# Step A of the first batch behind 22 idle matmuls, four of its groups in three fp32r parts, and no idle matmuls ahead of step D

## The chip, the cores and the metric

The kernel runs on one core of one Trainium2 chip. Its engines are TensorE (PE, with its weight loads shown as PEld), VectorE (DVE), ScalarE (ACT), GpSimd (POOL) and SyncE (SP, which here only issues DMAs). The metric is the device time of one execution in microseconds, and of several runs the median. Times inside a trace are counted from the first instruction of the span.

## What is computed

The reference mixes each sequence in the frequency domain and then runs a two-layer network over all tokens:

```python
X = np.fft.rfft(x, axis=1)                     # x: 4 x 3008 x 256
Yr = Xr @ w_r - Xi @ w_i + b_r
Yi = Xr @ w_i + Xi @ w_r + b_i
Yr = np.sign(Yr) * np.maximum(np.abs(Yr) - lam, 0.0)    # lam = 0.01, the same for Yi
y = np.fft.irfft(Yr + 1j * Yi, n=3008, axis=1)
h = y.reshape(12032, 256) @ w_in               # 256 x 2048
g = np.maximum(h, 0.0) + alpha * np.minimum(h, 0.0)
out = g @ w_out                                # 2048 x 256
```

## The kernel before

**The transform as matmuls.** 3008 = 47 x 64, so the transform and its inverse are each two short DFTs. For a batch b, step A (`a_load`, `a_mm`, `a_evac`) multiplies x by a 47-point table, in 16 groups g of two rows each (`NG = R // 2`). Step B (`b_load`, `b_mm`, `b_evac`, `b_evac2`) does the 64-point part for 12 pairs q, `m_mm` and `m_evac` mix the channels and shrink, step C (`c_mm`, `c_evac`) begins the inverse transform, and step D (`d_load`, `d_open`, `d_step`) ends it and leaves the tokens split into a high and a low fp32r part for the two layers (`l1_step`, `l2_step`), which fill the rest of the time.

**Two ways to multiply.** A product in full float32 is one call in the code and two matmul instructions in the trace. A product in fp32r needs its inputs split into a high and a low part (`split`: ACT copies the high part, another engine subtracts it) and is three instructions: high weight by high data, low weight by high data, high weight by low data. In `a_mm`, batches 0 and 1 take the first way with the table `lf_s` (L389), batches 2 and 3 the second with `la_s` (L392 to L394); for those `a_split` makes the parts `xh` and `xl`, each from two buffers.

**The head of the program** is written out by hand (from L988), and each engine runs its instructions in the order in which they are written. POOL issues the loads of `lf_s`, of the small tables for the bias (`first_bias`, L188 and L191) and of `la_s`. DVE clears the bias tiles (L194, L195) and then the tile `idle`. PE runs `keep_warm(36)`, which is 36 matmuls of 128 x 128 in bf16 of a tile of zeros, whose result nobody reads. SP issues the loads of x: a pair of groups (four rows) is two DMAs, one of 80 partitions and one of 14, and the first pair is four; behind them the tables `rb_s`, the first loads of batch 1 (`xt`), the mixing weights (`wm_f`) and the first raw layer weights (`cw_s`). SP has eight semaphores for its DMAs, so that the ninth DMA waits for the first to land.

**The loop over step A** runs over the 16 groups of batch 0 and the first four (`EARLY`) of batch 1:

```python
for n, (b, g) in enumerate(seq):
    a_mm(b, g)
    if n >= 1:
        a_evac(*seq[n - 1])
    if n == NG:
        for q in range(3):
            b_load(0, q)
```

In batch 0 `a_evac` puts even groups on ACT (L406) and odd ones on DVE (L404); `b_load` is two DMAs on POOL (L420). The products of a group stand in a PSUM tile of the pool `ps_f`, tag "f", which has three buffers: a group writes where the third group before it stood, and waits until that was read. `b_load(0, q)` needs all 16 groups of batch 0, the last of which DVE evacuates. Behind the loop stands `keep_warm(70)` (`WARM`), then the loop over the 12 pairs.

**Ahead of step D**, a list written out by hand (`TAIL`) ends step C, issues the first two loads of step D (`zt`) and fills PE with ten more groups of step A of batch 1; behind them come `keep_warm(12)` and the first two steps D. `d_step` takes two `ps_f` tiles, one for each half of the channels, and each becomes high and low parts on ACT and DVE (L139, L142).

Of the kernel before, what the change touches and what calls it, by code (L numbers as in the profile page):

```python
# [93 lines left out]
def fft_mix_moe(ctx, tc, x, w_r, w_i, b_r, b_i, w_in, w_out, alpha, la, rb, lc, rd, lf, cf, sel, out):  # L94
    nc = tc.nc
# [35 lines left out]
    V, G, A, PE = nc.vector, nc.gpsimd, nc.scalar, nc.tensor  # L131

    def f(t):
        return t.bitcast(F32)

    def split(src, hi, lo, e_hi, e_lo):

        if e_hi is A:
            A.activation(out=hi, in_=src, func=AF.Copy)  # L139
        else:  # L140
            e_hi.tensor_copy(out=hi, in_=src)
        e_lo.tensor_tensor(out=lo, in0=src, in1=f(hi), op=ALU.subtract)  # L142


    la_s = const.tile([NP, 2, NQ], F32R, name="la_s")
# [37 lines left out]
    def first_bias():  # L183

        raw = work.tile([4, 2, C], F32, tag="Yt", name="bias_f", bufs=1)
        hi = work.tile([4, 2, C], F32R, tag="Yc", name="bias_h", bufs=1)
        pick = work.tile([4, 129], F32, tag="ot", name="sel", bufs=1)
        nc.gpsimd.dma_start(out=pick, in_=sel)  # L188
        for i, b in enumerate((b_r, b_i)):
            for k in range(2):  # L190
                nc.gpsimd.dma_start(out=raw[2 * i:2 * i + 2, k], in_=b.unsqueeze(0).to_broadcast([2, C]))  # L191
        rows = const.tile([128, 2, C], F32R, tag="bias", name="bias_p")
        ones = const.tile([128, 128], F32R, tag="wd", name="ones")
        V.memset(f(rows), 0.0)  # L194
        V.memset(f(ones), 0.0)  # L195
        bias[0] = ones, rows

        def parts():
            V.memset(lam_s, -LAM)
            V.tensor_copy(out=ones[0:4], in_=pick[:, 0:128])  # L200
            V.tensor_copy(out=hi, in_=raw)
            V.scalar_tensor_tensor(out=rows[0:4], in0=f(hi), scalar=pick[:, 128:129], in1=raw, op0=ALU.mult, op1=ALU.add)

        return parts
# [9 lines left out]
    def load_rb(n0, n1):  # L214
        nc.sync.dma_start(out=rb_s[:, n0:n1], in_=rb[:, n0:n1])
# [10 lines left out]
    def split_mix():  # L226
        for t, w in zip(mix_w, mix):
            split(t, w[:, 0], w[:, 1], A, G)
        mix_w.clear()
# [24 lines left out]
    def conv_load():  # L254

        m, i = divmod(conv_m[0], 2)
        conv_m[0] += 1
        k = conv_m[0] % 3
        raw = cw_s[:, NSLOT + 8 * k:NSLOT + 8 * k + 8].rearrange("p (k n) f -> p k (n f)", k=2)
        raw = raw.rearrange("p k (n w) -> p k n w", w=2)  # L260
        src = w_out.bitcast(U32)[256 * m:256 * m + 256] if i else w_in.bitcast(U32)[:, 512 * m:512 * m + 512]
        nc.sync.dma_start(out=raw.rearrange("p k n w -> p k (n w)"), in_=src.rearrange("(k p) f -> p k f", p=128))
        conv_raw.append((raw, m, i))
# [77 lines left out]
    def a_load(b, g):  # L341

        if g == 0:
            ad[b] = dram.tile([NQ, R, C], F32, tag="ad", name=f"ad{b}")
        src = x[b].rearrange("(p r) c -> p r c", r=R)[:, 4 * g:4 * g + 4]
        if b == 0:
            ts = [x_s[:, 4 * g:4 * g + 4]]
        elif b == 1 and g in X1_TAGS:
            tags = X1_TAGS[g]
            ts = [work.tile([NP, 4 // len(tags), C], F32, tag=tag, name="xt", bufs={"Yl": None, "gh": 4}.get(tag, 1))  # L350
                  for tag in tags]
        else:
            ts = [work.tile([NP, 4, C], F32, tag="xt", name="xt")]
        if (b, g) == (0, 0):
            ts = [ts[0][:, 0:2], ts[0][:, 2:4]]
        n = 4 // len(ts)
        for i, t in enumerate(ts):

            for p in ((0, 80), (80, NP)):
                nc.sync.dma_start(out=t[slice(*p)], in_=src[slice(*p), n * i:n * i + n])  # L360
        xt[b, g] = ts

    def x_rows(b, g):
        ts = xt[b, g // 2]
        if len(ts) == 1:
            return [ts[0][:, 2 * (g % 2):2 * (g % 2) + 2]]
        n = len(ts) // 2
        return ts[n * (g % 2):n * (g % 2) + n]

    xp = {}  # L370

    def a_split(b, g):

        t, = x_rows(b, g)
        hi = work.tile([NP, 2, C], F32R, tag="xh", name="xh")
        lo = work.tile([NP, 2, C], F32R, tag="xl", name="xl")
        split(t, hi, lo, A, V)
        xp[b, g] = hi, lo
# [3 lines left out]
    def a_mm(b, g):  # L382
        ps = ps_f.tile([NQ, 2, C], F32, tag="f", name="ps_a")
        pa[b, g] = ps
        if b < 2:
            ts = x_rows(b, g)
            n = 2 // len(ts)
            for i, t in enumerate(ts):
                PE.matmul(ps[:, n * i:n * i + n], lf_s, t, start=True, stop=True)  # L389
            return  # L390
        hi, lo = xp.pop((b, g))
        PE.matmul(ps, la_s[:, 0], hi, start=True, stop=False)  # L392
        PE.matmul(ps, la_s[:, 1], hi, start=False, stop=False)
        PE.matmul(ps, la_s[:, 0], lo, start=False, stop=True)  # L394

    def a_evac(b, g):
        ps = pa.pop((b, g))
        if b == 0:
            st = a0_s[:, g]
        else:  # L400
            tag = A1_TAGS[g] if b == 1 and g < len(A1_TAGS) else "zst"
            st = work.tile([NQ, 2, C], F32, tag=tag, name="ast", bufs={"bt": 3, "zst": 3, "Yt": 1, "Yc": 1}.get(tag))
        if b == 0 and g % 2:
            V.tensor_copy(out=st, in_=ps)  # L404
        else:
            A.activation(out=st, in_=ps, func=AF.Copy)  # L406
        if b:
            stores.append((ad[b][:, 2 * g:2 * g + 2], st))
# [3 lines left out]
    def b_load(b, q):  # L412
        t = work.tile([128, 2, C], F32, tag="bt", name="bt", bufs=3)
        if b == 0:
            src = a0_s.rearrange("(w s q) g r c -> q w s (g r) c", w=4, s=2)[q]
        else:
            src = ad[b].rearrange("(w s q) r c -> q w s r c", w=4, s=2)[q]

        for k in range(2):
            (nc.gpsimd if b == 0 else nc.sync).dma_start(out=t[:, k], in_=src[:, k])  # L420
        bt[b, q] = t
# [549 lines left out]
    PAT = [0, 0] + [1] * 46  # L971
    NG = R // 2
    EARLY = 4
    FILL = 14
    C0 = 2
    PT = [1, 2, 3, 3, 3, 3, 3, 3, 3, 3, 4, 4]
# [4 lines left out]
    idle = const.tile([128, 128], BF16, name="idle")  # L981

    def keep_warm(n):
        ps = ps_f.tile([128, 512], F32, tag="f", name="ps_idle")
        for _ in range(n):
            PE.matmul(ps[:, 0:128], idle, idle, start=True, stop=True)

    with tc.manual_schedule():  # L988
        nc.gpsimd.dma_start(out=lf_s, in_=lf)
        bias_parts = first_bias()  # L990
        nc.gpsimd.dma_start(out=la_s, in_=la)
        V.memset(idle, 0.0)
        keep_warm(36)
        for g in range(NG // 2):
            a_load(0, g)
        load_rb(0, 4)
        for g in range(EARLY // 2):
            a_load(1, g)
# [3 lines left out]
        for _ in range(C0):  # L1002
            conv_load()
        seq = [(0, g) for g in range(NG)] + [(1, g) for g in range(EARLY)]

        for n, (b, g) in enumerate(seq):
            a_mm(b, g)
            if n >= 1:
                a_evac(*seq[n - 1])
            if n == NG:  # L1010
                for q in range(3):
                    b_load(0, q)
                split_mix()
                bias_parts()
# [9 lines left out]

        a1 = [EARLY]
        hold = []

        def a_fill(n):
            for g in range(a1[0], min(a1[0] + n, FILL)):
                a_mm(1, g)  # L1030
                a_evac(1, g)
                a1[0] = g + 1
# [38 lines left out]
                {"me": m_evac, "cm": c_mm, "ce": c_evac}[op](0, NPAIR - args[0])  # L1071
        V.tensor_scalar(out=beta_s, in0=alpha_s, scalar1=-1.0, scalar2=1.0, op0=ALU.mult, op1=ALU.add)
        conv_tags.update(v1=("xh", "xl"), ex=("Yh", "Yh"), lf=("Yl", "bt"))
        keep_warm(12)
        for c in range(2):
            d_open(c)
            d_step(0, c)
# [22 lines left out]
        for b in range(B):  # L1100
# [9 lines left out]
            if b == 0:  # L1110
                for g in range(FILL, NG):
                    i = 6 * (g - FILL) + 9
                    if g % 2 == 0:
                        at(i - 8, a_load, 1, g // 2)
                    at(i, a_mm, 1, g)
                    at(i, a_evac, 1, g)
            else:
                for g in range(NG if b + 1 < B else 0):
                    i = AO[b + 1] + 3 * g // 2
                    if g % 2 == 0:  # L1120
                        at(i - 5, a_load, b + 1, g // 2)
                    at(i - 2, a_split, b + 1, g)
                    at(i, a_mm, b + 1, g)
                    at(i, a_evac, b + 1, g)
# [73 lines left out]
        for k in range(len(spairs) + SLAG):  # L1198
# [9 lines left out]
            if k >= SLAG:  # L1208
                n, t = spairs[k - SLAG]
# [43 lines left out]
```

## Time and profile before

| What | us |
|---|---|
| Median of 3 runs (lowest, highest) | 1350.11 (1349.89, 1350.86) |
| The profiled execution | 1351.47 |
| Span of its trace, first to last instruction | 1349.7 |
| PE busy in it | 1334.4 |
| First idle matmul to first matmul of step A | 1.68 to 5.13 |
| First load of step B issued; its first matmul | 20.80; 28.57 |
| First matmul of step D | 101.22 |

The profile was taken in one execution. A row of its timeline gives the start and the length of a run of like instructions, their count, and in brackets how long the engine was idle before them and what ended that. PE's matmuls overlap: one of 512 columns in float32 is listed with some 0.59 us, but the next begins 0.43 us after it. The idle time of an engine that nobody waits for costs nothing.

### The profile page before, as it was taken

The numbers are of one execution on the slowest core, as the hardware profiler recorded it, in microseconds if no ns is written. First come the engines' busy times: TensorE is split into PE (matmuls) and PEld (weight loads), VectorE is DVE, ScalarE is ACT, GpSimd is POOL, SyncE is SP. The second block draws the span as 40 slices with busy tenths as digits, with TensorE's granted clock in tenths as the row PEclk, the third lists the DMA queues.
The fourth block names the chain that finished last, engine by engine and source line by source line (L and its number), as shares of the span: only waits on it lengthen the run. The fifth ranks groups of instructions, "written<-read, shape, count | busy, mean of one in ns | idle before, by whom it ended". The sixth has DMA issues, their size and how long they took to land.

```text
span 1349.7 us, 25116 instructions
## 1 busy us (share of the span) xinstructions
PE 1334.4 (99%) x9200; PEld 1250.5 (93%) x9200; DVE 1035.8 (77%) x1934; ACT 760.9 (56%) x1527; POOL 379.0 (28%) x403
## 2 busy tenths in 40 slices
PE   8999999999999999999999999999999999999998
PEld 5979999999999999999999999999999999999998
DVE  2767856776777777776778888888888888888885
ACT  3566655665565555555555555655555556555553
POOL 4854742222221222222121211121112112221222
PEclk9999999999999999999999999999999999999999
DMA  9964223342333312111110110111011101110001
GB/s 244 252 197 136 81 95 105 109 136 72 98 113 114 113 52 79 52 58 41 35 36 2 40 28 5 36 28 28 7 34 28 29 7 34 28 28 9 20 17 28
DMA packets 88117, 89.64 MB, mean 66 GB/s; under 512 B 42317, under 2 KB 70448, under 8 KB 87995
## 3 DMA queue, kind: packets, MB, share of 16 engines
q1 hardware_dynamic: 79700, 77.02, 20.0%
q0 software_dynamic: 5168, 8.02, 2.3%
q10 hardware_dynamic: 3127, 3.01, 0.7%
q8 instruction: 72, 1.18, 0.4%
q14 instruction: 50, 0.41, 0.1%
HBM read 50.49 MB, written 34.34 MB: 63 GB/s over the span
## 4 chain that ended last, share of the span: by engine, by line
PE 90%; DMA 3%; DVE 2%; issue 1%; ACT 1%; SPq 1%; POOL 0%; ACTq 0%; DVEq 0%; POOLq 0%
PE ps_h L791 24%; PE ps_h L686 14%; PE ps_m L488 6%; PE ps_o L893 6%; PE ps_o L894 6%; PE ps_o L892 6%; PE ps_d L617 4%; PE ps_o L725 3%; PE ps_o L724 3%; PE ps_o L723 3%; PE ps_b L428 2%; PE o_last L724 1%; PE o_last L725 1%; PE o_last L723 1%; PE o_last L892 1%; PE o_last L893 1%
## 5 line engine op out<-in xcount | busy, mean ns | idle before, releaser
L791 PE MATMUL ps_h<-yh,w 128*128 128x512 f32 (+1 forms) x960 | 315.6, 390 | 0.0
L830 POOL TENSOR_TENSOR l<-t,h 128x512 fp32r<-128x512 f32 x98 | 127.0, 1296 | 496.5 <-ACT h L828 456.6
L791 PEld LDWEIGHTS ps_h<-yh,w 128*128 128x128 f32 x960 | 180.0, 188 | 33.2
L795 DVE SCALAR_TENSOR_TENSOR sq<-sq,beta_s,ps_h 128x512 f32<-128x512 f32 (+1 forms) x240 | 168.0, 733 | 55.0 <-ACT sq L794 54.2
L686 PE MATMUL ps_h<-yh,w 128*128 128x384 f32 (+1 forms) x704 | 206.8, 336 | 0.9 <-DVE q L693 0.9
L791 PE MATMUL ps_h<-yl,w 128*128 128x512 f32 (+1 forms) x480 | 186.3, 388 | 0.0
L693 DVE SCALAR_TENSOR_TENSOR q<-q,beta_s,ps_h 128x384 f32<-128x384 f32 (+1 forms) x192 | 115.5, 602 | 85.3 <-ACT q L692 83.5
L697 ACT ACTIVATE gh<-q 128x384 fp32r<-128x384 f32 (+1 forms) x192 | 99.1, 516 | 144.5 <-DVE q L693 143.5
L698 POOL TENSOR_TENSOR gl<-q,gh 128x384 fp32r<-128x384 f32 (+1 forms) x90 | 96.6, 1074 | 263.2 <-ACT gh L697 256.4
L810 ACT ACTIVATE dh<-sq 128x768 fp32r<-128x768 f32 x112 | 94.7, 846 | 117.9 <-DVE sq L795 75.2
L794 ACT ACTIVATE sq<-ps_h 128x512 f32<-128x512 f32 (+1 forms) x240 | 133.1, 586 | 27.5 <-PE ps_h L791 23.1
L686 PEld LDWEIGHTS ps_h<-yh,w 128*128 128x128 f32 x704 | 129.4, 189 | 3.8 <-issue 0.8
L828 ACT ACTIVATE h<-t 128x512 fp32r<-128x512 f32 x98 | 62.0, 633 | 105.0 <-DVE t L826 101.7
L686 PE MATMUL ps_h<-yl,w 128*128 128x384 f32 (+1 forms) x352 | 116.5, 331 | 0.0
L692 ACT ACTIVATE q<-ps_h 128x384 f32<-128x384 f32 (+1 forms) x192 | 91.7, 478 | 42.5 <-PE ps_h L686 41.0
L725 PE MATMUL ps_o<-w,gl 128*128 128x256 f32 x384 | 108.0, 281 | 1.7 <-POOL gl L698 1.7
L724 PE MATMUL ps_o<-w,gh 128*128 128x256 f32 x384 | 107.8, 281 | 0.0
L723 PE MATMUL ps_o<-w,gh 128*128 128x256 f32 x384 | 107.7, 281 | 0.0
L791 PEld LDWEIGHTS ps_h<-yl,w 128*128 128x128 f32 x480 | 90.6, 189 | 13.6
L825 DVE TENSOR_TENSOR dl<-sq,dh 128x768 fp32r<-128x768 f32 x98 | 93.5, 954 | 3.8 <-ACT dh L810 3.8
L894 PE MATMUL ps_o<-l,sw_a 128*128 128x256 f32 x294 | 82.0, 279 | 0.0
L892 PE MATMUL ps_o<-h,sw_a 128*128 128x256 f32 x294 | 81.9, 279 | 0.0
(214 smaller groups left out, 3620.2 us busy)
## 6 DMA issues: line engine op xcount, KB each, us to landing
zt<-zd SPq DMA_DIRECT2D x32, 384.0 KB
zd<-zst SPq DMA_DIRECT2D x37, 256.0 KB
ad<-ast SPq DMA_DIRECT2D x48, 192.0 KB
bt<-ad SPq DMA_DIRECT2D x72, 128.0 KB
xt<-in_x SPq DMA_DIRECT2D x21, 320.0 KB
out<-oT SPq DMA_DIRECT2D x152, 32.0 KB
cw_s<-in_moe_w_in SPq DMA_DIRECT2D x8, 512.0 KB
cw_s<-in_moe_w_out SPq DMA_DIRECT2D x8, 512.0 KB
```

The source lines that it names most:

```text
L686: PE.matmul(ps, wi_h[m // FH][:, w, ct, 128 * (m % FH):128 * (m % FH) + 128], a[:, ct, 0:n], start=(k == 0), stop=(k == 3 * CT - 1))
L693: V.scalar_tensor_tensor(out=q, in0=q, scalar=beta_s[:, m:m + 1], in1=ps, op0=ALU.mult, op1=ALU.add)
L697: A.activation(out=hi, in_=q, func=AF.Copy)
L723: PE.matmul(a, hi[:, t], w[:, 0], start=(i, k) in first, stop=False)
L724: PE.matmul(a, hi[:, t], w[:, 1], start=False, stop=False)
L725: PE.matmul(a, lo[:, t], w[:, 0], start=False, stop=(i, k) in last)
L791: PE.matmul(ps, wi_h[m // FH][:, w, ct, 128 * (m % FH):128 * (m % FH) + 128], a[:, ct, 0:w1], start=(k == 0), stop=(k == 3 * CT - 1))
L794: A.activation(out=q[:, j], in_=ps, func=AF.Relu, scale=-1.0)
L795: V.scalar_tensor_tensor(out=q[:, j], in0=q[:, j], scalar=beta_s[:, m:m + 1], in1=ps, op0=ALU.mult, op1=ALU.add)
L830: G.tensor_tensor(out=l24, in0=t24, in1=f(h24), op=ALU.subtract)
L892: PE.matmul(o, wh, gh, start=first, stop=False)
L894: PE.matmul(o, wh, gl, start=False, stop=last)
```

## The change

The warm-up has 22 idle matmuls in place of 36, and `idle` is cleared first of all on DVE. The load of `la_s` moves up behind that of `lf_s`, ahead of the four bias loads and `sel`. Groups 9, 11, 13 and 15 of batch 0 are split while earlier groups run, two turns of the loop ahead, and multiplied in three fp32r parts; `a_mm` now tells the two ways apart by whether a split of the group exists. The twelve idle matmuls ahead of step D are gone.

```diff
@@ def a_mm(b, g)
-        if b < 2:
+        if (b, g) not in xp:
...
+    SPLIT = (9, 11, 13, 15)
...
+        V.memset(idle, 0.0)
         nc.gpsimd.dma_start(out=lf_s, in_=lf)
+        nc.gpsimd.dma_start(out=la_s, in_=la)
         bias_parts = first_bias()
-        nc.gpsimd.dma_start(out=la_s, in_=la)
-        V.memset(idle, 0.0)
-        keep_warm(36)
+        keep_warm(22)
...
             if n >= 1:
                 a_evac(*seq[n - 1])
+            if n + 2 in SPLIT:
+                a_split(0, n + 2)
...
-        keep_warm(12)
         for c in range(2):
             d_open(c)
             d_step(0, c)
```

On DVE, in step A of batch 0, the rows before are these: the evacuations (COPY) of groups 1 to 15, odd ones only, each out of the PSUM tile that its number names.

```order
L194 MEMSET bias_p_97 128x512
L195 MEMSET ones_98 128x128
L992 MEMSET idle_85 128x64
L404 COPY a0_83<-ps_a_176 96x512
L404 COPY a0_83<-ps_a_182 96x512
L404 COPY a0_83<-ps_a_188 96x512
L404 COPY a0_83<-ps_a_194 96x512
L404 COPY a0_83<-ps_a_200 96x512
L404 COPY a0_83<-ps_a_206 96x512
```

The same place now; `ps_a_180` is group 7, and `xl_184` is the low part of group 9.

```order
L990 MEMSET idle_85 128x64
L194 MEMSET bias_p_99 128x512
L195 MEMSET ones_100 128x128
L404 COPY a0_83<-ps_a_174 96x512
L142 TENSOR_TENSOR xl_184<-x0_82,xh_183 94x512
L404 COPY a0_83<-ps_a_180 96x512
L142 TENSOR_TENSOR xl_196<-x0_82,xh_195 94x512
L404 COPY a0_83<-ps_a_190 96x512
L142 TENSOR_TENSOR xl_208<-x0_82,xh_207 94x512
L404 COPY a0_83<-ps_a_202 96x512
L142 TENSOR_TENSOR xl_220<-x0_82,xh_219 94x512
L404 COPY a0_83<-ps_a_214 96x512
```

The clearing of `idle` has moved to the front, and the low parts of groups 9, 11, 13 and 15 stand ahead of the evacuations of groups 7, 9, 11 and 13. ACT has the same pattern: the high parts of those groups stand behind its evacuations of groups 6, 8, 10 and 12.

On PE, groups 7 to 12 of batch 0 before, one row for a group:

```order
L389 MATMUL ps_a_194<-x0_82,lf_s_73 96x512
L389 MATMUL ps_a_197<-x0_82,lf_s_73 96x512
L389 MATMUL ps_a_200<-x0_82,lf_s_73 96x512
L389 MATMUL ps_a_203<-x0_82,lf_s_73 96x512
L389 MATMUL ps_a_206<-x0_82,lf_s_73 96x512
L389 MATMUL ps_a_209<-x0_82,lf_s_73 96x512
```

The same groups now:

```order
L389 MATMUL ps_a_180<-x0_82,lf_s_73 96x512
L389 MATMUL ps_a_187<-x0_82,lf_s_73 96x512
L392 MATMUL ps_a_190<-xh_183,la_s_72 96x512
L393 MATMUL ps_a_190<-xh_183,la_s_72 96x512
L394 MATMUL ps_a_190<-xl_184,la_s_72 96x512
L389 MATMUL ps_a_199<-x0_82,lf_s_73 96x512
L392 MATMUL ps_a_202<-xh_195,la_s_72 96x512
L393 MATMUL ps_a_202<-xh_195,la_s_72 96x512
L394 MATMUL ps_a_202<-xl_196,la_s_72 96x512
L389 MATMUL ps_a_211<-x0_82,lf_s_73 96x512
```

Groups 9 and 11 have become three rows each, the last of which reads the low part that DVE makes; nothing has changed places.

## Rows read from the trace of the kernel before

**Rows 1.** Windows: busy us (count) of PE, PEld, DVE, ACT, POOL; clock, DMA share, GB/s.

```profile
31.50:62.50 31.00, 31.00 (x243) 30.14 (x243) 22.88 (x33) 16.80 (x29) 27.61 (x38) 1.00 0.98 238
```

**Rows 2.** Timeline of all engines from the start to 8 us.

```profile
0.92 0.48 DVE L194 MEMSET bias_p<- 128x512 f32 x1 [0.92 <-PEq L1233]
1.29 0.75 POOL L989 DMA_DIRECT2D lf_s<-tab_lf  x1 [0.84 <-POOLq L1233]
1.51 0.11 DVE L992 MEMSET idle<- 128x64 uint32 x1
1.68 3.62 PE L986 MATMUL ps_idle<-idle 128*128 128x128 bf16 x36 [1.68 <-DVE idle L992]
5.13 14.28 PE L389 MATMUL ps_a<-x,lf_s 94*96 94x512 f32 x32
7.15 0.24 PEld L389 LDWEIGHTS ps_a<-x,lf_s 94*96 94x96 f32 x2 [0.96 <-PE ps_a L389]
```

**Rows 3.** Chain that ended last, to 21.5 us: start, length, what.

```profile
4.22 5.45 DMA x<-in_x
9.69 6.48 DMA x<-in_x
```

**Rows 4.** Idle matmuls in two windows: count, ns min/median/max, first and last start.

```profile
L986 PE MATMUL ps_idle<-idle x27: 288/314/315, 1.7 to 4.4; 128*128 128x128 bf16 x27
L986 PE MATMUL ps_idle<-idle x7: 219/219/264, 4.6 to 5.0; 128*128 128x128 bf16 x7
```

**Rows 5.** DMA issues, 0 to 32 us: count, KB each, median us to landing.

```profile
la_s<-tab_la POOLq DMA_DIRECT2D x1, 70.5 KB, 6.8
lf_s<-tab_lf POOLq DMA_DIRECT2D x1, 35.2 KB, 2.9
```

**Rows 6.** Timeline of ACT and DVE: evacuations of groups 6, 7, 10 and 15.

```profile
11.72 0.59 ACT L406 ACTIVATE a<-ps_a 96x512 f32<-96x512 f32 x1 [1.12 <-PE ps_a L389]
12.58 0.69 DVE L404 COPY a<-ps_a 96x512 f32<-96x512 f32 x1 [1.03 <-PE ps_a L389]
15.15 0.59 ACT L406 ACTIVATE a<-ps_a 96x512 f32<-96x512 f32 x1 [1.12 <-PE ps_a L389]
19.45 0.69 DVE L404 COPY a<-ps_a 96x512 f32<-96x512 f32 x1 [1.03 <-PE ps_a L389]
```

**Rows 7.** Splits of batches 2 and 3: count, ns min/median/max, first and last start.

```profile
L139 ACT ACTIVATE xh<-xt x32: 614/618/625, 228.6 to 456.3; 94x512 fp32r<-94x512 f32 x32
L142 DVE TENSOR_TENSOR xl<-xt,xh x32: 680/689/690, 230.3 to 457.0; 94x512 fp32r<-94x512 f32 x32
```

**Rows 8.** Timeline of PE: a group in three parts, and what follows it.

```profile
451.25 0.39 PE L392 MATMUL ps_a<-xh,la_s 94*96 94x512 f32 x1
...
451.94 0.34 PE L686 MATMUL ps_h<-yh,w 128*128 128x384 f32 x1
```

**Rows 9.** DMA queues, 20.8 to 24 us (q1 SP's, q0 POOL's): packets, MB, share.

```profile
q1 hardware_dynamic: 579, 1.27, 102.6%
q0 software_dynamic: 26, 0.00, 0.5%
```

**Rows 10.** Timeline of POOL and PE up to step B.

```profile
20.80 4.10 POOL L420 DMA_DIRECT2D bt<-a  x6 [15.73 <-DVE bias_h L201]
...
23.94 4.07 PE L986 MATMUL ps_idle<-idle 128*128 128x128 bf16 x70
28.57 1.76 PE L428 MATMUL ps_b<-rb_s,bt 128*128 128x128 f32 x12 [0.55 <-issue]
31.00 0.71 PE L428 MATMUL ps_b<-rb_s,bt 128*128 128x128 f32 x4 [0.67 <-DMA bt<-a]
```

**Rows 11.** Timeline of PE, 100 to 108 us.

```profile
100.54 0.84 PE L986 MATMUL ps_idle<-idle 128*128 128x128 bf16 x12
101.22 2.87 PE L617 MATMUL ps_d<-rd_s,zt 96*128 96x94 f32 x24
104.41 1.10 PE L617 MATMUL ps_d<-rd_s,zt 96*128 96x94 f32 x8 [0.32 <-DVE hl L142]
```

## The prediction

> **What bounds the kernel now.** I read the busy shares by stage first, then PE's timeline up to the first layer, the chain of waits, and last the DMA queues. Once step B runs PE has no gap: from 31.5 to 62.5 us it is busy for all 31.0 us at full clock, with DMA busy 98% beside it [rows 1]. So the change, which touches only the first 20 us and one place at 100 us, is worth what it moves at two points: when PE can begin step B, and when it can begin step D. The reader should see that these have different limits. Step B begins late because of its loads: POOL issues them at 20.80, and PE waits 0.55 us before 28.57 and 0.67 us before 31.00 [rows 10], the second time by name for the DMA. Step D begins at 101.22 straight behind twelve idle matmuls that began at 100.54, with no wait between [rows 11].
>
> In front of step A stand three things: the idle matmuls from 1.68 to about 5.13 [rows 2], the table `lf_s`, issued at 1.29 [rows 2] and landed 2.9 us later, at 4.19 [rows 5], and the loads of x. Step A has 16 groups in 32 matmuls over 14.28 us [rows 2]; two passes of a group take 0.86 us start to start (14.28 less 0.3 us of wait, explained next, and 0.2 us of tail, by 16). The third group does not begin at 5.13 + 1.72 = 6.85 but at 7.15, after an idle weight loader [rows 2]: x was not there. The chain shows how x comes: a load issued at 4.22 lands at 9.67, and one issued at 9.69 lands at 16.17 [rows 3]. From the third group on the groups follow each other without a gap, since every 1.72 us of two groups takes a little longer than a pair of x takes to come; the evacuations show it, 12.58 (group 7) and 19.45 (group 15) being 6.87 us apart, eight times 0.86 [rows 6].
>
> **The shorter warm-up.** `idle` is cleared first, so at 0.92 + 0.11 in place of 1.62, and PE can begin at 1.09 [rows 2]. In the lower of its two clock levels an idle matmul follows the one before by 0.104 us ((4.4 - 1.7) / 26) and lasts 314 ns; from 4.6 us on it lasts 219 [rows 4], so the clock rose from 1.2 to 2.4 GHz there, while the matmuls ran back to back. 22 of them end at 1.09 + 22 x 0.105 = 3.4. Then step A waits for `lf_s` until 4.19, and its first group begins near 4.3, 0.85 us earlier than now. That buys nothing: the third group still needs its x, at 7.15. If the clock is at its upper level the two first groups are done by 6.0; if it stays low for both, they take 2 x 1.72 = 3.44 us and end at 7.72, which is 0.57 late. So this part is worth 0, with an end at 0.57 lost. A gain is excluded in this execution by the row at 7.15; in an execution whose clock rises later than here the old order would lose some tenths that the new one doesn't, as its step A begins sooner.
>
> What the rows show is that PE had no pause before the clock rose; the new order has one of 0.9 us, from 3.4 to 4.3. The Trainium skill, "TensorE: Matmul & The Clock Gate", section "What's actually happening", says that the low level is the default, that activity lifts it, and that the moment differs from run to run. The trace agrees on the level at the start (314 ns, then 219); no run here shows what a pause does before the rise. By that rule the 0.57 or more is the likelier end, and the rival "late clock" below is what it would do.
>
> **`la_s` first.** Its 70.5 KB [rows 5] are issued some 2.5 us earlier and share the DMA engines with the second and third pair of x. At 238 GB/s [rows 1] that is 0.30 us. The bias tables come later by one issue, and nobody needs them before step A is over. The delay is 0 to 0.3 us at the third group, and goes through to the end of step A because the groups have no gap. I take 0.1, since `la_s` is spread over 6.8 us to landing [rows 5].
>
> **Four groups in three parts.** On PE three parts take 451.94 - 451.25 = 0.69 us [rows 8] for 0.86: four groups save 4 x 0.17 = 0.68, which is the lower end. But each split puts 0.62 us on ACT and 0.69 on DVE [rows 7], and the order puts the low part of group 9 ahead of DVE's evacuation of group 7. I follow that. ACT ends the evacuation of group 6 at 11.72 + 0.59 = 12.31, the high part of group 9 at 12.93, DVE its low part at 13.67 (0.05 us of handover). The evacuation of group 7, now at 12.58 [rows 6], begins at 13.67 and ends at 14.36. Group 10 writes where group 7 stood, so it begins at 14.40; today it began at 14.09 (its evacuation at 15.15 [rows 6], less 1.06, the distance between a group's start and its evacuation's). The same again: evacuation of 10 from 15.46 to 16.05, high part of 13 to 16.67, low part to 17.41, evacuation of 11 to 18.10, group 14 at 18.14. That turn takes 18.14 - 14.40 = 3.74 us for four groups; four in full float32 take 3.44. Groups 14 and 15 then take 0.86 + 0.69, and the evacuation of group 15 begins at 18.14 + 1.55 + 0.2 = 19.9 in place of 19.45. So the split makes step A later by 0.45 us, not earlier: the evacuations take PE's place as its bound. I take +0.45, because the orders of DVE and ACT are fixed and their durations are rows.
>
> **From step A to step B.** The six loads of step B are issued 0.45 + 0.1 = 0.55 us later, at 21.35. What that costs at 28.57 and 31.00 lies between 0 and 0.55. For 0 speaks that between 20.8 and 24 us queue 1 holds the engines (102.6%) while POOL's queue 0 moves 26 packets of next to nothing (0.5%) [rows 9]: the loads stand there whether they come at 20.8 or 21.3. For 0.55 speaks that once they move, six loads follow each other. PE also runs 70 idle matmuls until 28.01 [rows 10], so it could not use an earlier landing beyond 0.55 us. I take the middle, +0.3. The Trainium skill, "DMA: Bandwidth & Descriptors", section "Queues, rings and completion order", says that a DMA engine takes turns between the queues that have work. The 0.5% of queue 0 doesn't look like turns; by that rule the loads would get their share from the start, the delay would go through whole, and the sum below would be -0.13 in place of -0.4.
>
> **No idle matmuls ahead of step D.** Step D begins at 100.54 in place of 101.22: -0.68. PE has no pause there, so nothing is warmed. The first load of step D must be there 0.68 us sooner. The trace doesn't name the landing; but 24 matmuls of step D run in 2.87 us from 101.22 with no wait [rows 11], 0.11 us each, so that the second load had landed by its first use, 16 matmuls later, at 103.0, and it would now be used at 102.3. The ends are -0.68 and 0. The removed tile also shifts the turn of the three buffers by one: the second step's first half now follows the last group of step A in its buffer, which ACT reads by 101.4, ahead of 102.3. The wait at 104.41 for DVE [rows 11] depends on step D's own first products and moves along. I take -0.68.
>
> **The sum.** 0 + 0.3 - 0.68 = -0.4 us. The profiled execution took 1351.47 us for a span of 1349.7, so it would take 1351.1; the median of the runs shown is 1350.11, and so I say **1349.7**. About 0.2% (2.7 us) is what a measurement of this kernel can tell from no change, and the whole reach of the change is smaller than that.
>
> **Rivals.** (1) *Splits pay.* If DVE and ACT fit the splits into their idle time (an evacuation is preceded by some 1.0 us of it [rows 6]) and group 10 doesn't wait, step A ends 0.68 sooner, and half to all of it reaches step B: -0.68 - 0.34 to -0.68 - 0.68, about **1348.9**. Against it stands the order, low part ahead of evacuation. (2) *Late clock*, the one that ends slower than before: the pause between the idle matmuls and step A keeps the clock low through the first two groups, so that all later groups shift by 0.57. With 0.45 and 0.1 that is 1.1 us at the issue of step B's loads, too much to hide behind queue 1; it passes whole and the sum is +1.1 - 0.68 = +0.4, **1350.5**. It decides from a delay of 0.68 at step B; each further microsecond at the low level adds 0.5. For it speaks the pause, against it that 22 matmuls came before. (3) *Step D gains nothing*, because its loads or the chain through DVE end the wait anyway: +0.3, **1350.4**. For it speaks the wait at 104.41, against it that the start at 101.22 has none.
>
> **How the numbers follow.** Forecast 0.5 (its own range 1349.3 to 1350.0), splits pay 0.17, late clock 0.18, step D gains nothing 0.12, none of these 0.03. Adding the 0.4 us to either side by which single runs stand from the median (1349.89 to 1350.86), rival 1 reaches 1348.5; rival 2 with another microsecond of low clock reaches 1351.0. The range is **1348.5 to 1351.1**. No case comes near 2.7 us: faster by over 0.2% has 0.04, slower 0.03, within 0.2% 0.93.
>
> **What would show it.** In the changed profile: idle matmuls from 1.1 to 3.4, step A from 4.3, its third group still near 7.2 (late clock: near 7.7 or later, with long matmuls before); DVE's row of `xl` directly ahead of an evacuation without idle time between, and group 10 near 14.4; the last evacuation on DVE near 19.9 to 20.1; the loads of step B at 21.3 and its first matmuls near 28.8; step D directly behind step A of batch 1, and its wait for DVE of 0.3 us still there. The forecast is wrong if the last evacuation of step A comes before 19.4, if the third group starts after 7.5, or if PE waits ahead of step D.

## The result and the profile after

The changed kernel takes **1362.39 us** (four runs, 1361.62 to 1363.29) beside 1350.0 us (1349.61 to 1350.86) for the kernel before: a ratio of 1.0086 [1.0073, 1.0099], slower by 12.4 us. The forecast was 1349.7 with a range to 1351.1. The profiled execution of after (1361.62 us) has a span of 1359.5 us, 9.8 more than the 1349.7 of before (1351.47 us); the rest of the 12.4 lies in how single executions stand from their median.

PE's timeline of after, in three windows (start, length, engine, line, operation, count, idle time before and what ended it; a row that reaches the end of its window is cut there, with its length and count). The first up to the end of step A of batch 0:

```profile
1.00 2.53 PE L987 MATMUL ps_idle<-idle 128*128 128x128 bf16 x22 [1.00 <-DVE idle L990]
4.51 15.68 PE L389 MATMUL ps_a<-x,lf_s 94*96 94x512 f32 x18 [0.99 <-DMA lf_s<-tab_lf]
19.20 1.42 PE L392 MATMUL ps_a<-xh,la_s 94*96 94x512 f32 x1
20.41 0.63 PE L393 MATMUL ps_a<-xh,la_s 94*96 94x512 f32 x1
20.84 0.63 PE L394 MATMUL ps_a<-xl,la_s 94*96 94x512 f32 x1
21.26 1.91 PE L389 MATMUL ps_a<-x,lf_s 94*96 94x512 f32 x2
22.18 1.42 PE L392 MATMUL ps_a<-xh,la_s 94*96 94x512 f32 x1
```

Then the early groups of batch 1, the 70 idle matmuls, step B and the first mixing:

```profile
30.22 7.03 PE L389 MATMUL ps_a<-xt,lf_s 94*96 94x512 f32 x8
37.04 4.53 PE L987 MATMUL ps_idle<-idle 128*128 128x128 bf16 x70
41.41 2.00 PE L428 MATMUL ps_b<-rb_s,bt 128*128 128x128 f32 x16
43.17 0.48 PE L468 MATMUL ps_m<-bias_p,ones 128*128 128x512 f32 x1
```

And the place ahead of step D:

```profile
102.43 8.76 PE L389 MATMUL ps_a<-xt,lf_s 94*96 94x512 f32 x24
111.03 2.81 PE L617 MATMUL ps_d<-rd_s,zt 96*128 96x94 f32 x24
114.16 1.10 PE L617 MATMUL ps_d<-rd_s,zt 96*128 96x94 f32 x8 [0.32 <-DVE hl L142]
```

The head stands where it was expected: idle matmuls from 1.00, step A from 4.51. But its groups take twice as long. The groups of step A by tile, after from 4.4 to 30 us and then before from 7.9 to 17 us (count, ns min/median/max, first and last start):

```profile
L389 PE MATMUL ps_a<-x,lf_s x24: 1055/1061/1167, 4.5 to 28.1; 94*96 94x512 f32 x24
```

```profile
L389 PE MATMUL ps_a<-x,lf_s x22: 592/592/593, 7.7 to 16.7; 94*96 94x512 f32 x22
```

In after no float32 pass of step A is shorter than 1055 ns; before, they take 592. The idle matmuls tell which level of the clock that is. The three groups of them in after, by tile:

```profile
L987 PE MATMUL ps_idle<-idle x22: 288/314/314, 1.0 to 3.2; 128*128 128x128 bf16 x22
```

```profile
L987 PE MATMUL ps_idle<-idle x9: 274/314/314, 37.0 to 37.9; 128*128 128x128 bf16 x9
```

```profile
L987 PE MATMUL ps_idle<-idle x61: 219/219/223, 38.0 to 41.4; 128*128 128x128 bf16 x61
```

The 22 in front of step A take 288 to 314 ns, as at the lower level in [rows 4], and the first nine of the 70 behind it 274 to 314; from 38.0 us on they take 219. So TensorE's clock stayed at 1.2 GHz through the whole of step A, until 38.0 us; before, it rose at 4.6 us [rows 4]. PE did not rest meanwhile. Windows of after (busy us and count of PE, PEld, DVE, ACT, POOL; the clock on record, DMA share, GB/s):

```profile
4.60:36.90 32.30, 32.30 (x44) 12.13 (x45) 9.11 (x16) 9.63 (x17) 5.45 (x8) 1.00 0.73 196
43.20:95.00 51.80, 51.62 (x393) 49.20 (x392) 42.61 (x58) 30.02 (x52) 45.23 (x58) 1.00 0.93 240
```

PE is busy for 32.30 of 32.30 us. The clock column reads 1.00 there because no record of a lower level stands in the trace ahead of the first rise; the level has to be read from the lengths of the matmuls. The start of the first record is the rise, 38.00 us in after; where a rise is given below, it is this start.

**Where the 9.8 us of the profile come from.** From the first group of step A to the idle matmuls behind it, after takes 37.04 - 4.51 = 32.5 us, before 23.94 - 5.13 = 18.8 [rows 2, 10]. Along the path:

| Event, start in us | before | after | difference |
|---|---|---|---|
| First group of step A | 5.13 | 4.51 | -0.6 |
| Last evacuation of batch 0 on DVE | 19.45 | 30.46 | +11.0 |
| Loads of step B issued | 20.80 | 31.81 | +11.0 |
| Step B on PE | 28.57 | 41.41 | +12.8 |
| First mixing matmul (L468) | 31.47 | 43.17 | +11.7 |
| Step D | 101.22 | 111.03 | +9.8 |

The rows of after for the last evacuation and for the loads:

```profile
30.46 0.69 DVE L404 COPY a<-ps_a 96x512 f32<-96x512 f32 x1 [1.83 <-PE ps_a L394]
31.81 4.11 POOL L420 DMA_DIRECT2D bt<-a  x6 [26.75 <-DVE bias_h L201]
```

Step B is now held back by PE's own queue, the 70 idle matmuls, and not by its loads, so the two waits of [rows 10] are gone. From the mixing to step D, 1.9 us come back: 0.68 are the idle matmuls taken out, and the rest are waits of PE that are shorter (one of 0.74 us at 64.28 is gone, one of 0.82 at 84.71 has become 0.31 at 95.18). Behind step D nothing changes: +9.8 there and +9.8 at the end.

### The profile page after: what moved, and what is told of

Its sections match the earlier page's. It is cut to its first block, busy times and chain, and to the rows that moved or that the text cites. A ratio compares the mean times of both kernels' runs of the same rounds, so it can differ in the third digit from the quotient of the medians.

```text
span 1359.5 us, 25089 instructions
## 1 busy us (share of the span) xinstructions
PE 1347.5 (99%) x9178; PEld 1254.9 (92%) x9178; DVE 1037.9 (76%) x1938; ACT 763.5 (56%) x1531; POOL 379.7 (28%) x403
## 4 chain that ended last, share of the span: by engine, by line
PE 94%; DVE 2%; DMA 1%; ACT 1%; issue 1%; POOL 0%; ACTq 0%; SPq 0%; POOLq 0%; DVEq 0%
PE ps_h L791 24%; PE ps_h L686 13%; PE ps_m L488 6%; PE ps_o L893 6%; PE ps_o L894 6%; PE ps_o L892 6%; PE ps_d L617 4%; PE ps_o L725 3%; PE ps_o L724 3%; PE ps_o L723 3%; PE ps_a L389 3%; PE ps_b L428 3%; PE o_last L724 1%; PE o_last L725 1%; PE o_last L723 1%; PE o_last L892 1%
## 5 line engine op out<-in xcount | busy, mean ns | idle before, releaser
L791 PE MATMUL ps_h<-yh,w 128*128 128x512 f32 (+1 forms) x960 | 315.6, 389 | 0.0
L791 PEld LDWEIGHTS ps_h<-yh,w 128*128 128x128 f32 x960 | 180.0, 188 | 33.2
L791 PE MATMUL ps_h<-yl,w 128*128 128x512 f32 (+1 forms) x480 | 186.2, 388 | 0.0
L791 PEld LDWEIGHTS ps_h<-yl,w 128*128 128x128 f32 x480 | 90.5, 189 | 13.6
```

Source lines behind the costliest of these rows:

```text
L791: PE.matmul(ps, wi_h[m // FH][:, w, ct, 128 * (m % FH):128 * (m % FH) + 128], a[:, ct, 0:w1], start=(k == 0), stop=(k == 3 * CT - 1))
```

## The experiments

Each study has its own runs of the kernel before beside it (medians 1351.8, 1351.73 and 1351.57 of 31, 25 and 26), so the ratios are to be compared, not the medians. Four of the kernels below fall into two groups of executions, with 10 to 13 us between them and no run there. I call an execution *late* where it belongs to the upper group. Five profiles of late executions were taken (after, e1, e4, e5, e6), and in all five the clock rises only among the 70 idle matmuls, between 37.5 and 42.2 us; in the profiles that were not late it rises by 9.7 us at the latest. So a share of late executions is a share in which the clock stayed low through step A. Of the 82 runs of the kernel before, none is late (the highest is 1355.65).

**Is it the warm-up?** First the number alone in the kernel before, then the old number alone in after.

```diff
@@ the kernel before
-        keep_warm(36)
+        keep_warm(22)
```

> The kernel before with 22 idle matmuls in place of 36 and nothing else changed; they run from 1.7 to 4.0 us, and step A follows as soon as its table has landed at 4.2, so the pause ahead of it is only 0.2 us. Theory 'too few idle matmuls' (the clock had not yet risen when step A began, and step A's own float32 matmuls do not lift it): step A runs at the low clock to its end, the clock rises only in the 70 idle matmuls ahead of step B, near 38 us, and the time is 8 to 13 us over the kernel before. Theory 'pause' (the 1.0 us without a matmul ahead of step A undid what the idle matmuls had done): with the pause nearly gone the clock rises near 5 us and the time is within 1 us of the kernel before.

Measured: two groups, 1350.79 to 1354.05 and 1364.84 to 1365.91, five runs of ten in each; ratio over all of them 1.0052 [1.0019, 1.0084]. The profile is of a late execution. PE's timeline from the start, then the 70 idle matmuls in two windows by tile:

```profile
1.68 2.53 PE L986 MATMUL ps_idle<-idle 128*128 128x128 bf16 x22 [1.68 <-DVE idle L992]
4.25 5.44 PE L389 MATMUL ps_a<-x,lf_s 94*96 94x512 f32 x6
```

```profile
L986 PE MATMUL ps_idle<-idle x34: 314/314/314, 38.5 to 42.0; 128*128 128x128 bf16 x34
```

```profile
L986 PE MATMUL ps_idle<-idle x35: 219/219/220, 42.2 to 44.1; 128*128 128x128 bf16 x35
```

The idle matmuls end at 1.68 + 2.53 = 4.21 and step A begins at 4.25, and still the clock stays low. So the number alone is enough; neither the splits nor the pause are needed. Its late executions are some 3 us longer than after's (1365 against 1362). Part of this is that at the low level the splits pay, since two groups take 21.26 to 24.25 = 2.99 us in after with one of them in three parts, and 2 x 1.71 = 3.41 without: 1.7 us for the four. Part is the twelve idle matmuls ahead of step D that e1 still has, and in its profile the clock also rises later, at 42.2 us in place of 38.0.

```diff
@@ after
-        keep_warm(22)
+        keep_warm(36)
```

> The changed kernel with 36 idle matmuls in place of 22, which fill the time from 1.0 to 4.6 us and leave no pause. Both theories of the clock: it rises before step A's third group, step A runs at the high clock and the time falls back by 10 to 13 us to about that of the kernel before. What is left of the change by my prediction: step A's last evacuation 0.4 us later by the splits, step B 0 to 0.5 later, step D 0.68 sooner, so 0.2 to 0.7 us under the kernel before. If splitting pays, about 1 us under.

Measured: 1350.1 to 1354.25, no late run in ten, ratio 1.0 [0.9991, 1.001]. PE's timeline:

```profile
1.00 4.02 PE L987 MATMUL ps_idle<-idle 128*128 128x128 bf16 x36 [1.00 <-DVE idle L990]
4.81 4.55 PE L389 MATMUL ps_a<-x,lf_s 94*96 94x512 f32 x8
```

With 36 the whole loss is gone. The 14 idle matmuls that the change took away are its cause; all else in the change together is worth 0 +/- 1.3 us. The rise itself need not come among them: in this profile all 36 run at the low level (286 to 311 ns), and the clock rises at 6.34 us, in the second group of step A.

**Pause, moment or length?** Three kernels change what PE does ahead of step A. In e3 the 22 come later, so that no pause is left (DVE makes three other clears first); in e4, 14 run ahead of a pause and 22 behind it; e5 is after itself again.

```diff
@@ e3, on after
-        V.memset(idle, 0.0)
...
         bias_parts = first_bias()
+        V.memset(f(bias[0][1]), 0.0)
+        V.memset(idle, 0.0)
@@ e4, on after (keep_warm takes the tile as a second argument)
-        keep_warm(22)
+        for _ in range(3):
+            V.memset(f(bias[0][1]), 0.0)
+        V.memset(idle2, 0.0)
+        keep_warm(14)
+        keep_warm(22, idle2)
```

> The changed kernel with its 22 idle matmuls started later (the tile idle is cleared behind three other clears on DVE), from about 2.2 to 4.5 us, so that step A follows them without a pause. 'Too few': still 8 to 13 us slower than the kernel before, clock up only near 38 us. 'Pause': within 1 us of the kernel before.

> The changed kernel with 36 idle matmuls again, but a pause in them: 14 from 1.0 us, then none for about 0.7 us (they read a second tile that DVE clears later), then 22 to about 5.5 us, straight into step A. 'Too few': 36 are enough, the clock rises before or in the first groups of step A, time within 1.5 us of the kernel before. 'Pause': the last stretch is again 22 matmuls behind a pause, so the clock stays low and the time is 8 to 13 us over.

> The changed kernel itself, for the share of its executions in which the clock stays low. The runs so far fall in two groups, near 1351 us and near 1363 to 1367 us, the second with the clock low until the 70 idle matmuls ahead of step B. Theory 'chance': with 22 idle matmuls the clock rises in time in some executions and not in others, and the pause does not matter: of ten, 3 to 7 in the slow group, as with 22 idle matmuls and hardly a pause. Theory 'pause': 22 and a pause of 1.0 us fail in nearly all, 9 or 10 of ten.

Measured: e3 four late runs of ten (1362.67 to 1363.67, the others 1350.7 to 1352.62), ratio 1.0034 [1.0006, 1.0063]; e4 three of ten (1365.41 to 1367.09, the others 1349.93 to 1352.27), ratio 1.0014 [0.9982, 1.0045]; e5 four of four (1361.68 to 1364.08), ratio 1.0076 [1.0061, 1.0091]. With the first result, after is late in eight of eight. The profile of e3 caught an execution that is not late: PE's timeline, and its passes of step A by tile in two windows.

```profile
2.22 2.53 PE L987 MATMUL ps_idle<-idle 128*128 128x128 bf16 x22 [2.22 <-DVE idle L994]
4.54 2.87 PE L389 MATMUL ps_a<-x,lf_s 94*96 94x512 f32 x4
```

```profile
L389 PE MATMUL ps_a<-x,lf_s x3: 684/1061/1114, 4.5 to 6.3; 94*96 94x512 f32 x3
```

```profile
L389 PE MATMUL ps_a<-x,lf_s x10: 592/592/641, 7.9 to 11.8; 94*96 94x512 f32 x10
```

Here step A begins at the low level too, and its passes fall from 1061 to 592 ns at about 6.5 us. So in these kernels it is decided by chance whether the clock rises by the first two groups; in the five late profiles, where it did not, it did not rise in any group behind either. After is late in eight of eight, e1 and e3 together in nine of twenty. They differ from after in the pause, but also in that their idle matmuls begin 0.7 and 1.2 us later, and which of the two makes the difference is not told apart; doing away with the pause is no cure in any case. In e4 as many idle matmuls as in the kernel before, with a pause in the middle, are not as good as 36 in a row (three of ten against none of 82).

**How many, and is it the count?** e6 has 28. e7 keeps 22 but makes each twice as wide. e8 puts 22 more behind the first group.

```diff
@@ e6, on after
-        keep_warm(22)
+        keep_warm(28)
@@ e7, on after
-    idle = const.tile([128, 128], BF16, name="idle")
+    idle = const.tile([128, 256], BF16, name="idle")
-    def keep_warm(n):
+    def keep_warm(n, w=128):
...
-            PE.matmul(ps[:, 0:128], idle, idle, start=True, stop=True)
+            PE.matmul(ps[:, 0:w], idle[:, 0:128], idle[:, 0:w], start=True, stop=True)
...
-        keep_warm(22)
+        keep_warm(22, 256)
@@ e8, on after
             a_mm(b, g)
+            if n == 0:
+                keep_warm(22)
```

> The changed kernel with 28 idle matmuls, which end near 4.0 us, so that the pause ahead of step A is 0.2 us. Theory 'chance, by the length of the stretch of idle matmuls': a share of slow executions between that of 22 (4 or 5 of ten) and that of 36 (0 of ten), so 1 to 3 of ten; the fast ones within 1 us of the kernel before. Theory 'pause': no slow ones, since there is none left.

> The changed kernel with 22 idle matmuls of 256 columns in place of 128, so the same count for twice the time, from 1.0 to about 5.5 us at the low clock. If the time of the idle stretch counts: no slow execution of ten, times within 1 us of the kernel before (step A begins near 5.0 to 5.7 us, its third group needs its data at 7.1 anyway). If the number of matmuls counts: slow in about half, as with 22.

> The changed kernel with 22 more idle matmuls behind the first group of step A. If idle matmuls lift the clock wherever they stand, together with those in front: at most 1 slow execution of ten, the fast ones 0 to 1.5 us over those of the kernel before, because the second group begins 1.2 to 2.4 us later. If only one long stretch does: slow in a fifth to a half of the executions, as each stretch of 22 has its own chance.

Measured: e6 three late runs of ten (1362.53 to 1362.86, the others 1349.48 to 1352.8), ratio 1.0013 [0.9988, 1.0039]; e7 none of ten (1349.43 to 1351.77), ratio 0.9989 [0.998, 0.9998]; e8 none of ten (1350.64 to 1354.1), ratio 1.0005 [0.9996, 1.0014]. PE's timeline of e7, and its idle matmuls by tile:

```profile
1.06 4.87 PE L987 MATMUL ps_idle<-idle 128*128 128x256 bf16 x22 [1.06 <-DVE idle L990]
5.73 3.65 PE L389 MATMUL ps_a<-x,lf_s 94*96 94x512 f32 x7
```

```profile
L987 PE MATMUL ps_idle<-idle x22: 392/417/417, 1.1 to 5.5; 128*128 128x256 bf16 x22
```

The same 22 instructions, spread over 4.9 us and not 2.5, have the clock up in time in every execution: the count alone does not decide it. Each matmul is also twice as much work, so whether the length or the work counts is not told apart. e8 shows that it can also be lifted behind the first group, a little later (9.63 us in its profile) and at no measurable loss. In one table, by what PE does up to step A:

| Idle matmuls ahead of step A | Length, us | Late executions |
|---|---|---|
| 22, then 0.8 to 1.0 us of pause (after, e5) | 2.5 | 8 of 8 |
| 22, no pause (e1; e3) | 2.5 | 5 of 10; 4 of 10 |
| 28, then 0.3 us of pause (e6) | 3.2 | 3 of 10 |
| 14, 0.9 us of pause, 22 (e4) | 1.7 + 2.5 | 3 of 10 |
| 22, 0.7 us of pause, first group, 22 more (e8) | 2.5 + 2.6 | 0 of 10 |
| 36 (before; e2; e9; e10) | 3.4 to 4.0 | 0 of 82; 0 of 10; 0 of 11; 0 of 11 |
| 22 of 256 columns (e7; e11) | 4.9; 4.8 | 0 of 10; 0 of 11 |

**The other parts by themselves,** with eleven executions of each, since less than 2 us is at stake. e9 is the kernel before without the idle matmuls ahead of step D; e10 is the kernel before with the splits; e11 is e7 without the splits.

```diff
@@ e9, on before
-        keep_warm(12)
@@ e10, on before
-        if b < 2:
+        if (b, g) not in xp:
...
+    SPLIT = (9, 11, 13, 15)
...
+            if n + 2 in SPLIT:
+                a_split(0, n + 2)
@@ e11, on e7
-    SPLIT = (9, 11, 13, 15)
+    SPLIT = ()
```

> The kernel before without the twelve idle matmuls ahead of step D, nothing else changed. My prediction: step D follows step A of batch 1 directly and everything behind it is 0.68 us earlier, so 0.68 us (0.05%) under the kernel before; if step D waits there for its loads or for DVE, 0.

> The kernel before with groups 9, 11, 13 and 15 of batch 0 in three fp32r parts, nothing else changed. My prediction: group 10 starts near 14.4 us, group 14 near 18.1, the last evacuation of step A near 19.9 in place of 19.45, and step B 0 to 0.5 us later, so 0 to 0.5 us over the kernel before. Rival, splits pay: the last evacuation 0.7 us earlier and 0.3 to 0.7 us under.

> The changed kernel with 22 idle matmuls of 256 columns and without the splits, so that of the change only the early clear of the idle tile, the place of la_s and the missing idle matmuls ahead of step D are left. If splitting costs 0 to 0.5 us, this is 0 to 0.5 us under the same kernel with the splits (1350.2 us where the kernel before had 1351.7); if splitting pays, 0.3 to 0.7 us over it. No slow executions in either case.

Measured: e9 0.9988 [0.9979, 0.9997], so -1.6 us (-2.8 to -0.4); e10 1.0009 [1.0, 1.0018], so +1.2 (0 to +2.4); e11 0.9988 [0.9979, 0.9997]. PE's timeline of e9 at the place:

```profile
96.73 4.04 PE L389 MATMUL ps_a<-xt,lf_s 94*96 94x512 f32 x13
100.60 2.81 PE L617 MATMUL ps_d<-rd_s,zt 96*128 96x94 f32 x24
103.74 1.10 PE L617 MATMUL ps_d<-rd_s,zt 96*128 96x94 f32 x8 [0.32 <-DVE hl L142]
```

Step D follows step A at once, 0.62 us ahead of [rows 11], and the span is 0.8 shorter. Step B of e10, PE's timeline:

```profile
29.43 1.13 PE L428 MATMUL ps_b<-rb_s,bt 128*128 128x128 f32 x8 [0.18 <-issue]
30.86 0.68 PE L428 MATMUL ps_b<-rb_s,bt 128*128 128x128 f32 x4 [0.31 <-DMA bt<-a]
32.34 0.71 PE L428 MATMUL ps_b<-rb_s,bt 128*128 128x128 f32 x4 [0.80 <-DMA bt<-a]
```

Its loads are issued at 21.71, 0.91 later than in [rows 10], and step B's last four matmuls begin 1.34 later. Part of that is not the splits: in this execution the clock rose at 6.9 us, against 4.7 in before, and so group 10 (14.96), group 14 (18.53) and the last evacuation (20.36) all come some 0.5 us behind what was expected of e10. e7 and e11, the same kernel with and without the splits, both with step A from 5.73, are the cleaner pair. They differ by 0.28 us at that issue (21.53 and 21.25) and by nothing measurable in the ratio. e7 and e11 are both faster than the kernel before; neither is measurably better than e9, which has one line of the change alone.

## Why the prediction was wrong

**The shorter warm-up (worth 0, end 0.57 lost): the step that failed.** The starts were right (1.00 and 4.51 for 1.1 and 4.3). The step let the clock stay low "for both" of the first groups at most, and so bounded the loss by two groups at the low level. It entered the sum as 0, with 0.57 as its end; the loads of step B came 11.0 us later, and step D 9.8. Nothing in the trace of before gave that bound: [rows 4] shows the clock rising among idle matmuls, and no row shows it rising under step A. In after it did not rise under step A at all. The third group began at 8.03, worse than the 7.72 of the bad end, and every float32 group behind it took 1.71 us in place of 0.86.

**Rival 2, late clock: right mechanism, wrong size.** The rival named the place, the cause and the rule of 0.5 us for each microsecond at the low level, and was then stopped after two groups, at +0.4 us. Carried on to the end of the stretch, the rule gives 32.5 x 0.5 = 16.3 us at the idle matmuls behind step A; the two stretches differ by 32.5 - 18.8 = 13.7, since the kernel before does not run through its own without waits (20 groups of 0.86 us are 17.2 of its 18.8) and has no fp32r parts in it. What counted for the chances was not the pause alone: e1 shows half of the executions late without one. "Against it that 22 matmuls came before" was an argument from a number of matmuls, and e7 shows that the number alone does not decide.

The Trainium skill, "TensorE: Matmul & The Clock Gate", section "What's actually happening", has the low level as the default, lifted by activity, at a moment that differs from run to run. The runs agree on the low level at the start (286 to 314 ns for idle matmuls of 128 columns) and on the chance (five of ten in e1). That the activity of step A would then lift it did not hold in after, with 32.30 busy us of float32 and fp32r passes and no rise.

The prediction itself called "the 0.57 or more" the likelier end by that rule, and yet put 0 into its sum, 0.57 into the rival and 0.18 on the rival's chance.

**`la_s` first (+0.1).** Not seen, and too small to be seen in single profiles. SP's load of `rb_s`, which waits for a load of x to land, is issued at 11.59 to 12.36 us in the four profiles with the old order (before, e1, e9, e10) and at 11.43 to 12.65 in the nine with the new one: executions of one order differ by more than the 0 to 0.3 in question.

**The splits (+0.45).** The walk through DVE and ACT held, where it can be compared. DVE's timeline of e2:

```profile
13.23 0.69 DVE L142 TENSOR_TENSOR xl<-x,xh 94x512 fp32r<-94x512 f32 x1 [1.31 <-ACT xh L139]
13.84 0.68 DVE L404 COPY a<-ps_a 96x512 f32<-96x512 f32 x1
...
19.12 1.41 DVE L404 COPY a<-ps_a 96x512 f32<-96x512 f32 x2
```

The low part stands directly ahead of the evacuation of group 7, as expected (13.84 for 13.67). PE's groups 10 and 14 in e2:

```profile
14.45 1.10 PE L389 MATMUL ps_a<-x,lf_s 94*96 94x512 f32 x2
...
18.01 1.10 PE L389 MATMUL ps_a<-x,lf_s 94*96 94x512 f32 x2
```

They stand at 14.45 and 18.01 for 14.40 and 18.14, and the last evacuation begins at 19.84 (the end of the row of two at 19.12, less one copy) for 19.9. That these absolute times agree is partly luck: in e3, e7 and e10, where the clock rose or step A began at other moments, group 10 stands at 14.79 to 14.96. What stays is the turn of four groups, 3.56 or 3.57 us in all five profiles at the upper level with splits (e2, e3, e7, e8, e10), over 3.44 without them, as the walk said; but it had 3.74. It added up listed lengths, and ACT and DVE begin the next instruction up to 0.1 us before the listed end of the one before (13.23 + 0.69 = 13.92 against 13.84 above). So the term was 0.29 in place of 0.45, by the last evacuations of e7 (20.19, the second of the two) and of e11:

```profile
19.46 1.42 DVE L404 COPY a<-ps_a 96x512 f32<-96x512 f32 x2
19.90 0.69 DVE L404 COPY a<-ps_a 96x512 f32<-96x512 f32 x1 [1.03 <-PE ps_a L389]
```

At the upper level the splits don't pay; rival 1 is out. For what they cost the whole kernel there are two measurements, nothing (e7 against e11) and 1.2 us (0 to 2.4, e10).

**From step A to step B (+0.3 of 0.55).** Inconclusive. The first matmul of step B comes 7.7 to 8.7 us behind the issue of its loads in before (28.57 - 20.80), e3, e7, e9, e10 and e11, and 6.6 and 6.0 us in e2 and e8, where it stands straight behind the 70 idle matmuls and a later one waits for the loads. The first mixing matmul, behind all of these waits, comes 9.3 (e8) to 11.1 us (e10) behind the issue. So executions differ here by 1.8 us, and neither the middle nor either end of the 0.55 is shown.

The page "DMA: Bandwidth & Descriptors" of the Trainium skill, section "Queues, rings and completion order", has a DMA engine take turns between the queues that have work. By that rule, the prediction said, the delay would go through whole; no run here shows whether it does.

**No idle matmuls ahead of step D (-0.68).** Right: -0.62 at step D in e9, and the wait for DVE moved along, as expected. Rival 3 is out. The interval of e9's time, -2.8 to -0.4, contains -0.68.

**The sum and the range.** Without the warm-up, the sum of -0.4 us is within what e2 (-1.2 to +1.4) and e7 (-2.7 to -0.3) allow. The range failed because the one term with a step in it was entered as a small slope.

## What to carry to other kernels

In this kernel idle matmuls at the start buy a level of the clock, and with fewer of them it is not a little less that is bought: the whole stretch behind them, 33 us, ran at half the speed, in some executions (e1) or in all (after). Before such a warm-up is shortened, ask which work behind it has been seen to lift the clock, and price the case in which none does, up to the next place where it is known to rise. One profile of a kernel near that edge says nothing of its chance: it takes some ten executions. And a warm-up is not described by its number of matmuls: 22 wide ones (e7) did here as well as 36 narrow ones, and 22 narrow ones did not.

## What the runs showed that was not expected

- PE was busy without a gap for 32.3 us (after, 4.6 to 36.9) at 1.2 GHz; the idle bf16 matmuls behind that had the clock up 0.5 us (e6) to 3.7 us (e1, 38.5 to 42.2) after their start. Once it is up, passes of step A keep it: in before they take 592 ns from 7.7 to 16.7 us, with no idle matmul between. And in e2, e3, e7, e8 and e10 the rise itself comes under passes of step A, 0.4 (e7) to 1.7 us (e3) behind the end of the last idle matmul. What it is in the two kinds of matmul (type, shape, weight loads) that makes them differ was not tried.
- The clock can also fall far from the start. In the profile of e2 it falls behind a wait of PE for POOL of 1.74 us at 166.62. Windows of e2 (columns as above):

```profile
160.00:166.70 6.70, 4.96 (x40) 4.76 (x38) 5.56 (x7) 3.88 (x10) 6.49 (x5) 1.00 0.00 0
166.80:170.10 3.30, 3.30 (x13) 3.30 (x14) 1.32 (x4) 0.60 (x2) 3.03 (x3) 0.50 0.02 5
170.30:176.00 5.70, 5.70 (x43) 5.70 (x41) 2.39 (x5) 3.06 (x6) 1.82 (x2) 1.00 0.00 0
```

  For 3.3 us it is granted at 0.50, which costs about 1.5 us: 2.0 us of lead at step D (99.18 against 101.22) have become 0.6 at the first matmul of L791 (683.11 against 683.69). The profile of e8 shows the same at 170 us; the other eleven profiles have a like wait of 1.68 to 1.74 us (1.71 at 168.70 in before, 1.74 at 178.50 in after) and keep the clock. What makes the difference was not tried.
